# Softmax sums of four head pairs in one matmul group, and their inverses spread by broadcast DMAs

## The chip, the cores and the metric

The kernel runs on one core of one Trainium2 chip. The metric is the device time in microseconds (us) of one execution; three executions of the kernel before took 481.07, 482.66 and 483.11 us, so its median is 482.66 us. A profile is taken of one further execution.

## The reference

Linformer attention on 8 batches, 8 heads, 1024 tokens and head size 64, followed by a feed-forward layer with a squared ReLU (8192 tokens, 512 features, 2048 hidden):

```python
k_proj = einsum('ks,bhsd->bhkd', E, k)             # 1024 keys projected to 64
v_proj = einsum('ks,bhsd->bhkd', F, v)
scores = q @ k_proj.T / sqrt(64)
attn   = exp(scores - max) / (sum(exp(scores - max)) + 1e-9)
x      = (attn @ v_proj) as (8192, 512)
h      = maximum(x @ w_in, 0)
out    = (h * h) @ w_out
```

The kernel leaves out the maximum, which changes nothing of the quotient, and computes the inverse of a sum as exp(-ln(sum)) on ScalarE (ACT).

## The kernel before

**Attention.** A batch has four head pairs. For each, `scores` (L352) makes four 64x64 matmuls into a PSUM tile of two banks (`ps_att`) and ACT writes the exponentials into `expT` (L343, four buffers). The 64 keys of a head lie on 64 partitions, so the softmax sum runs over partitions: a matmul with a matrix of ones gives it. `sums` and `sums_spread` do this for two pairs at once (eight matmuls, 64 rows by 32 columns), which leaves each sum on 32 partitions, 32 copies of one row. The multiply in `values` (L396, L409) needs it on 64. In `sums` (batch 0's second half and batch 1) ACT makes the inverse twice and VectorE (DVE) copies 32 partitions four times (L373). In `sums_spread` (batches 2 to 7) ACT makes `inv` once (L386, L387) and eight DMAs of SyncE's queue copy `inv` into two tiles `rs` of 128 partitions (L393), each from 32 partitions to 32. `inv` and `rs` share one tag with three buffers.

**Feed-forward.** Both products of a chunk of 512 tokens are done as seven half-size products in place of eight, with sums of the operands made on DVE (`sum_x`, `sum_h`), PSUM copies on ACT (L544, L662, L677) and sums with a kept product on DVE (L666). Kept products are tiles `u` of `part_pool`, finished rows are tiles `o_sb` of `out_pool`, stored by SyncE (L566).

**Order.** The order on TensorE (PE) is written out by hand; on the other engines a scheduler places instructions by program order and by when it takes them to be ready. From chunk (1, 1) on a loop of steps runs: each step is one first-layer product (four matmuls of 128x256, L652) and one second-layer quantum (four, L572). A batch has 56 steps. `on(t + n, b, name)` hangs an attention stage behind step n of a batch's period. In the loop there is one PSUM pair for attention, so its stages follow each other through it. Of batch b+2, counted from the period of batch b, the kernel before has: `transpose_q_dma` at 2, `project` at 30, `transpose_k_dma` at 32, `scores` at 44, 47 and 53 and at 1 of the next period, `sums_spread` at 50 and at 3 of the next period; there `values` follow at 7, 10, 20 and 23 and both `sum_x` at 24. Q of a further batch is loaded at 3, K and V at 34, on GpSimd's (POOL) queue.

```python
on(t + 44, b + 2, "scores", 0)
on(t + 47, b + 2, "scores", 1)
on(t + 50, b + 2, "sums_spread", 0)
on(t + 53, b + 2, "scores", 2)
```

Batch 1's attention runs inside chunk (0, 1), batch 2's scores inside chunk (1, 0) (`first_plain`, 16 steps).

Of the kernel before, what the change touches and what calls it, by code (L numbers as in the profile page):

```python
# [9 lines left out]
P = 128  # L10
F32 = mybir.dt.float32
BF16 = mybir.dt.bfloat16
AF = mybir.ActivationFunctionType
ALU = mybir.AluOpType
PE = mybir.EngineType.PE
LO, HI = slice(0, 64), slice(64, 128)
# [3 lines left out]
def kernel(  # L20
# [11 lines left out]
    nc = tc.nc  # L32

    B, H, S, D = q.shape
# [3 lines left out]
    DM = moe_w_out.shape[1]  # L38
# [6 lines left out]
    TCH = S // 2  # L45
# [10 lines left out]
    const_pool = ctx.enter_context(tc.tile_pool(name="const", bufs=1))  # L56
# [4 lines left out]
    soft_pool = ctx.enter_context(tc.tile_pool(name="soft", bufs=3))  # L61
    x_pool = ctx.enter_context(tc.tile_pool(name="x", bufs=2))
    form_pool = ctx.enter_context(tc.tile_pool(name="form", bufs=1))
    part_pool = ctx.enter_context(tc.tile_pool(name="part", bufs=5))
    out_pool = ctx.enter_context(tc.tile_pool(name="outp", bufs=3))
    psum = ctx.enter_context(tc.tile_pool(name="ps", bufs=1, space=bass.MemoryType.PSUM))
    turn = {"att": 0, "bank": 0, "pairs": 2}

# [6 lines left out]
    def att_psum():  # L75
        turn["att"] += 1
        return pair_psum(turn["att"] % turn["pairs"])

    def bank(shape=(P, 512), dtype=F32, n=None):
        if n is None:  # L80
            turn["bank"] += 1
            n = turn["bank"]
        return psum.tile(list(shape), dtype, tag=f"bank{n % 4}", name="ps_bank")
# [34 lines left out]
    nc.vector.memset(zeros[:], 0.0)  # L118
    ones = const_pool.tile([P, D], BF16, name="ones")
    nc.vector.memset(ones[:], 1.0)  # L120


    W_IN_PIECES = ((0, 2), (2, 4), (4, 8), (8, 12), (12, 16))
# [3 lines left out]
    for j, (lo, hi) in enumerate(W_IN_PIECES):  # L127
        t = wpool.tile([P, NCB, (hi - lo) * P], BF16, name=f"w_in_{lo}")
# [6 lines left out]
    for j in range(WP):  # L135
        if j == WP - 1:
            load(Q0[:, :, 4:8, :], tokens(q, 0, i=slice(4, 8)))
        t = wpool.tile([P, fn, DM], BF16, name=f"w_out_{j}")
# [81 lines left out]
    VALUE_QUADS = ((LO, 0, 0, LO), (HI, 0, 1, HI), (HI, 1, 1, LO), (LO, 1, 0, HI))  # L220

    class Attention:
# [31 lines left out]
        def project(self):  # L254
            ps = att_psum()[:, 0]
            for i in range(NI):
                f, l = i == 0, i == NI - 1
                nc.tensor.matmul(ps[LO, :], lhsT=ET[:, i, :], rhs=self.K[:, :, i, :], start=f, stop=l)
                nc.tensor.matmul(ps[HI, :], lhsT=FT[:, i, :], rhs=self.V[:, :, i, :], start=f, stop=l)
            for g in range(2):  # L260
                self.keep_k(ps[LO, g * C // 2:(g + 1) * C // 2], g)
            self.keep_v(ps[HI, :])
# [91 lines left out]
            self.scores_mm(ps, pr, slice(0, NT))  # L354
            self.e[pr] = self.exponentials(ps)

        def sums(self, pr):

            ps = att_psum()
            for j in range(2):  # L360
                for o, par, a, r in VALUE_QUADS:
                    c = 32 * (2 * a + j)
                    nc.tensor.matmul(
                        ps[c:c + 32, par], lhsT=ones[r, 0:32], rhs=self.e[pr + j][r, par], start=True, stop=True
                    )
            rs = [soft_pool.tile([P, 2, TCH], F32, tag="rs", name="rs") for _ in range(2)]
            nc.scalar.activation(rs[1][:], ps[:], AF.Ln)
            nc.scalar.activation(rs[0][:], rs[1][:], AF.Exp, scale=-1.0)
            nc.scalar.activation(rs[1][:], rs[1][:], AF.Exp, scale=-1.0)
            for j in range(2):  # L370
                for a in range(2):
                    have, lack = 32 * (2 * a + j), 32 * (2 * a + 1 - j)
                    nc.vector.tensor_copy(rs[j][lack:lack + 32], rs[j][have:have + 32])  # L373
                self.rs[pr + j] = rs[j]

        def sums_spread(self, pr):

            ps = att_psum()
            for j in range(2):
                for o, par, a, r in VALUE_QUADS:  # L380
                    c = 32 * (2 * a + j)
                    nc.tensor.matmul(
                        ps[c:c + 32, par], lhsT=ones[r, 0:32], rhs=self.e[pr + j][r, par], start=True, stop=True
                    )
            inv = soft_pool.tile([P, 2, TCH], F32, tag="rs", name="inv")
            nc.scalar.activation(inv[:], ps[:], AF.Ln)  # L386
            nc.scalar.activation(inv[:], inv[:], AF.Exp, scale=-1.0)  # L387
            for j in range(2):
                rs = soft_pool.tile([P, 2, TCH], F32, tag="rs", name="rs")
                for a in range(2):  # L390
                    have = 32 * (2 * a + j)
                    for to in (64 * a, 64 * a + 32):
                        nc.sync.dma_start(rs[to:to + 32], inv[have:have + 32])  # L393
                self.rs[pr + j] = rs

        def values(self, pr, spare=False):  # L396

# [40 lines left out]
    class Chunk:  # L438
# [100 lines left out]
                        yield  # L539


        def keep(self, ps):
            u = part_pool.tile([P, DM], F32, name="u")
            nc.scalar.copy(u[:], ps)  # L544
            return u

# [31 lines left out]
        def second_spread(self, second_bank):  # L578
# [21 lines left out]
            yield  # L600
            yield from product(7, chain)
            self.put(1, 1, chain, p5)
            yield
            yield from product(3, other)
# [6 lines left out]
        def second_seven(self, first, chain, other, last=False):  # L611
# [16 lines left out]
            yield  # L628
            yield from product(7, chain)
            self.put(1, 1, chain, p5)  # L630
            yield
            yield from product(3, other)
# [10 lines left out]
    class Group:  # L643
# [35 lines left out]
        def p5(self):  # L679
            self.other = bank(n=turn["bank"] + 2)  # L680
            self.product(5, self.other, True)
            self.kept5 = self.chunk.keep(self.other[:])

        def p6(self):
            self.product(6, self.chain)
            self.u2 = self.chunk.keep(self.chain[:])

        def p2(self):
            self.product(2, self.first)
# [18 lines left out]
    with tc.manual_schedule(engines={PE}):  # L708
# [30 lines left out]
        def at(step, fn, *args, **kwargs):  # L739
            plan.setdefault(step, []).append(lambda: fn(*args, **kwargs))  # L740

        def run(steps, start=0):
            for step, _ in enumerate(steps, start + 1):
                for stage in plan.pop(step, []):
                    stage()
            return step

        def run_all(*parts):
            step = 0
            for part in parts:  # L750
                step = run(part, step)
            assert not plan, plan

        atts = {0: att}
        chunk = {(0, c): Chunk(att, c) for c in range(2)}
# [7 lines left out]
        nxt = atts[1]  # L763
# [23 lines left out]
        at(44, nxt.transpose_q, 2)  # L787
        at(44, nxt.transpose_q, 3)
        at(44, lambda: atts[2].load_q())
        at(45, nxt.sums, 0)  # L790
        at(47, nxt.scores, 2)
        at(49, nxt.scores, 3)
        at(50, nxt.values, 0)
        at(52, nxt.values, 1)
        at(53, nxt.sums, 2)
        at(59, nxt.values, 2)
        at(60, nxt.values, 3)
        at(60, chunk[1, 1].sum_x)
# [5 lines left out]
        run_all(chunk[0, 0].first_cold(), chunk[0, 0].second_cold(), chunk[0, 1].first_plain(), chunk[0, 1].second_seven(*(bank()[:] for _ in range(3))))  # L804

        nxt = atts[2]
        at(1, nxt.transpose_k)
        at(3, nxt.scores, 0)
        at(5, nxt.scores, 1)
        at(7, nxt.sums_spread, 0)  # L810
        at(9, nxt.scores, 2)
        at(11, nxt.scores, 3)
        turn["pairs"] = 1
        run_all(chunk[1, 0].first_plain())
        lent.close()
        second_pool = ctx.enter_context(tc.tile_pool(name="ps_second", bufs=1, space=bass.MemoryType.PSUM))
# [37 lines left out]
        def both():  # L854
            f, s = firsts(), seconds()
            for _ in f:
                next(s, None)
                yield

        def on(step, b, name, *args):  # L860
            at(step, lambda: getattr(atts[b], name)(*args))

        for b in range(1, B - 1):
            t = 56 * (b - 1)
            if b > 1:
                on(t + 1, b + 1, "scores", 3)
            on(t + 3, b + 1, "sums_spread", 2)
            on(t + 7, b + 1, "values", 0)
            on(t + 10, b + 1, "values", 1)
            on(t + 20, b + 1, "values", 2)  # L870
            on(t + 23, b + 1, "values", 3)
            for c in range(2):
                at(t + 24, lambda b=b, c=c: chunk[b + 1, c].sum_x())
            if b + 2 < B:
                on(t + 2, b + 2, "transpose_q_dma")
                if b + 3 < B:
                    at(t + 2, begin, b + 3)
                    on(t + 3, b + 3, "load_q")
                on(t + 30, b + 2, "project")
                on(t + 32, b + 2, "transpose_k_dma")  # L880
                if b + 3 < B:
                    on(t + 34, b + 3, "load_kv")
                on(t + 44, b + 2, "scores", 0)
                on(t + 47, b + 2, "scores", 1)
                on(t + 50, b + 2, "sums_spread", 0)
                on(t + 53, b + 2, "scores", 2)
        steps = both()
        run(steps)
        assert not plan, plan
# [31 lines left out]
```

## Time and profile before

| | |
|---|---|
| median of three executions | 482.66 us |
| profiled execution, device time | 482.35 us |
| its span, first to last instruction | 480.5 us |
| PE busy | 470.4 us, 98% |
| DVE busy | 350.7 us, 73% |
| ACT busy | 287.2 us, 60% |
| one period of 56 steps (186.65 to 242.50, 242.50 to 298.35, 298.35 to 354.20) | 55.85 us each |
| DMA, mean rate | 139 GB/s |
| DMAs from `inv` to `rs` | 96, 128 KB each, 2.8 us from issue to landing (median; 2.2 to 8.9) |

Matmuls are pipelined, and the profile models their ends, so the busy share of PE is an upper bound of its work. Shares and counts are of one execution. A wait is put down to the event that came last.

### The profile page before, as it was taken

Reading aid. Unit: us, or ns where it says so; the run is one execution under the profiler, and the core shown is the slowest. Engines: PE = TensorE matmul, PEld = TensorE weight load, DVE = VectorE, ACT = ScalarE, POOL = GpSimd, SP = SyncE. Lnnn points to the kernel's source line nnn. Section 1 sums busy time; section 2 is a strip of 40 time slices with the busy share of each in tenths; the row PEclk is TensorE's granted clock in tenths of the full one; section 3 lists DMA queues with packets and bytes.
Section 4 is the critical chain, followed back from the end, with each engine's and each line's share of the span. In section 5 each row is a group of like instructions: output and inputs, shape, how many; then the busy total and the mean of one; then the engine's idle time right before and its main releaser. Section 6 shows DMA issues by size and latency. Waiting matters only on the chain.

```text
span 480.5 us, 10027 instructions
## 1 busy us (share of the span) xinstructions
PE 470.4 (98%) x4106; PEld 351.5 (73%) x4106; DVE 350.7 (73%) x613; ACT 287.2 (60%) x466; POOL 32.4 (7%) x45
## 2 busy tenths in 40 slices
PE   8999999999999999999999999999999999999996
PEld 3444445537878788787878778887887778888885
DVE  2456897956996679767897579966797678967671
ACT  2464467397547774678546785477745775565641
POOL 7310010200010000100010000100000000000000
PEclk9999999999999999999999999999999999999999
DMA  9999998999949496767939499495811054101012
GB/s 184 204 205 206 221 164 150 168 230 189 197 86 168 122 201 163 119 134 186 196 103 182 93 220 175 96 160 139 203 56 55 23 132 111 67 23 67 24 65 89
DMA packets 80046, 66.98 MB, mean 139 GB/s; under 512 B 30720, under 2 KB 76032, under 8 KB 80000
## 3 DMA queue, kind: packets, MB, share of 16 engines
q0 software_dynamic: 30640, 29.23, 39.4%
q1 hardware_dynamic: 49216, 36.97, 29.2%
q8 instruction: 32, 0.52, 0.4%
q10 hardware_dynamic: 144, 0.13, 0.1%
q14 instruction: 14, 0.11, 0.1%
HBM read 59.24 MB, written 16.78 MB: 158 GB/s over the span
## 4 chain that ended last, share of the span: by engine, by line
PE 71%; DVE 22%; ACT 3%; issue 2%; DMA 1%; DVEq 0%; ACTq 0%
PE ps_bank L652 28%; PE ps_second L572 27%; PE ps_bank L489 6%; DVE h L150 3%; DVE x_sum L150 3%; DVE h L666 3%; DVE s L150 2%; PE ps_att L329 2%; DVE xT L409 2%; PE ps_second L549 2%; PE ps_att L405 2%; DVE kp L246 1%; DVE rs L373 1%; DVE kp L247 1%; DVE w_in_sum L150 1%
## 5 line engine op out<-in xcount | busy, mean ns | idle before, releaser
L150 DVE TENSOR_TENSOR h<-h 128x1024 bf16<-128x1024 bf16 (+1 forms) x182 | 108.0, 616 | 39.1 <-ACT h L662 25.4
L652 PE MATMUL ps_bank<-x_sum,w_in_sum 128*128 128x256 bf16 x624 | 93.9, 273 | 0.0
L652 PEld LDWEIGHTS <-w_in_sum 128*128 128x128 bf16 x832 | 78.7, 98 | 16.2 <-issue 7.5
L572 PEld LDWEIGHTS <-h 128*128 128x128 bf16 x832 | 80.8, 98 | 10.6 <-DVE h L150 0.2
L662 ACT ACTIVATE h<-ps_bank 128x512 bf16<-128x512 f32 x104 | 62.9, 605 | 28.5 <-PE ps_bank L652 28.3
L544 ACT COPY u<-ps_bank 128x512 f32<-128x512 f32 x107 | 63.2, 591 | 26.6 <-PE ps_bank L652 23.6
L666 DVE CUSTOM_DVE_ANT_0 h<-ps_bank,u 128x512 bf16<-128x512 f32 x104 | 68.9, 685 | 13.0 <-PE ps_bank L652 12.5
L652 PEld LDWEIGHTS <-w_in 128*128 128x128 bf16 x624 | 58.8, 98 | 16.2 <-issue 9.5
L677 ACT COPY ps_bank<-ps_bank 128x512 f32<-128x512 f32 x52 | 29.7, 570 | 66.1 <-PE ps_bank L652 66.1
L572 PEld LDWEIGHTS <-s 128*128 128x128 bf16 x624 | 61.0, 98 | 7.1
L652 PE MATMUL ps_bank<-xT,w_in 128*128 128x256 bf16 x416 | 62.5, 273 | 0.0
L572 PE MATMUL ps_second<-w_out_sum,s 128*128 128x256 bf16 x416 | 62.4, 273 | 0.0
L572 PE MATMUL ps_second<-w_out_sum,h 128*128 128x256 bf16 x416 | 62.2, 273 | 0.0
L572 PE MATMUL ps_second<-w_out,h 128*128 128x256 bf16 x416 | 60.3, 273 | 0.0
L409 DVE TENSOR_TENSOR xT<-ps_att,rs 128x512 bf16<-128x512 f32 x56 | 36.0, 684 | 15.9 <-PE ps_att L405 15.9
L489 PE MATMUL ps_bank<-xT,w_in 128*128 128x512 bf16 x192 | 45.3, 379 | 1.8 <-DVE xT L434 1.0
L485 ACT ACTIVATE h<-ps_bank 128x512 bf16<-128x512 f32 x48 | 28.1, 606 | 16.1 <-PE ps_bank L489 15.9
L150 DVE TENSOR_TENSOR o_sb<-ps_second,u 128x512 f32<-128x512 f32 x27 | 18.5, 684 | 25.9 <-PE ps_second L572 20.7
L489 PEld LDWEIGHTS <-w_in 128*128 128x128 bf16 x192 | 17.7, 98 | 24.6 <-issue 6.2
L343 ACT ACTIVATE expT<-ps_att 128x1024 bf16<-128x1024 f32 x32 | 32.9, 1036 | 2.9 <-PE ps_att L329 2.5
L652 PE MATMUL ps_bank<-x_sum,w_in 128*128 128x256 bf16 x208 | 31.4, 273 | 1.4 <-DVE h L666 1.4
L652 PE MATMUL ps_bank<-xT,w_in_sum 128*128 128x256 bf16 x208 | 31.3, 273 | 0.0
(104 smaller groups left out, 477.2 us busy)
## 6 DMA issues: line engine op xcount, KB each, us to landing
out_dram<-o_sb SPq DMA_DIRECT2D x63, 256.0 KB, 2.4
rs<-inv SPq DMA_DIRECT2D x96, 128.0 KB, 2.8
K_sb<-in_k_dram POOLq DMA_DIRECT2D x7, 1024.0 KB, 9.5
V_sb<-in_v_dram POOLq DMA_DIRECT2D x7, 1024.0 KB, 15.8
Q_sb<-in_q_dram POOLq DMA_DIRECT2D x7, 1024.0 KB, 12.6
w_out<-in_moe_w_out_dram POOLq DMA_DIRECT2D x4, 512.0 KB, 17.9
w_in<-in_moe_w_in_dram POOLq DMA_DIRECT2D x3, 512.0 KB, 15.0
k_f<-in_k_dram SPq DMA_DIRECT2D x1, 512.0 KB, 4.9
```

Of the source, the lines that this page charges most:

```text
L150: return nc.vector.tensor_tensor(out=o, in0=x, in1=y, op=op)
L329: nc.tensor.matmul(ps[o, par], lhsT=self.kT[r, h % 4, h // 4, :], rhs=self.qT[r, h, n, :], start=True, stop=True)
L343: nc.scalar.activation(e[:], ps[:], AF.Exp, scale=SCALE)
L409: nc.vector.tensor_tensor(out=self.xT[:, pr, :, par], in0=ps_x[par].rearrange("p (c t) -> p c t", c=2), in1=rs[:, par].rearrange("p (c t) ...
L485: nc.scalar.activation(h, ps.rearrange("p (a t) -> p a t", a=2), AF.Relu)
L489: nc.tensor.matmul(ps[:], lhsT=w_in_blk(cb, fb), rhs=self.xT[:, cb, self.c].rearrange("p a t -> p (a t)"), start=(cb == 0), stop=(cb == NC ...
L544: nc.scalar.copy(u[:], ps)
L572: nc.tensor.matmul(ps[:, i * HM:(i + 1) * HM], lhsT=self.h_form(n, fb)[:, i * P:(i + 1) * P], rhs=w_out_form(n, fb), start=fresh and i == ...
L652: nc.tensor.matmul(ps[:, j * HC:(j + 1) * HC], lhsT=w_in_form(n, cb, 2 * self.g + j), rhs=self.chunk.x_form(n, cb), start=fresh and j == 0 ...
L662: nc.scalar.activation(self.out(kh, a), ps[:], AF.Relu)
L666: nc.vector._custom_dve(TENSOR_ADD_SAT, out=self.out(kh, a), in0=ps[:], in1=more[:], s0=3.0e38, s1=0.0)
L677: nc.scalar.copy(self.chain[:], self.first[:])
```

## The change

Sums of all four pairs of a batch are made together (`sums_all`): 16 matmuls whose left operand `pick` has 16 columns of ones and 16 of zeros, two of them accumulated into each block of 32 partitions, so that a sum lies on 16 partitions. One `Ln` and one `Exp` make one tile `inv`, which has a tag of its own with one buffer. `spread` then fills `rs` with four DMAs a pair. Each reads one row of `inv` (one partition, 512 floats) 64 times and writes 64 partitions. Batch 1's first two pairs use the same DMAs in place of the copies on DVE (`sums(0, True)`). The plan of the steps is changed with it: all scores stand ahead of the sums, `project` and `transpose_k_dma` move to 49 and 50, K and V are loaded there, Q at 26, `values` go to 6, 9, 19 and 22, the second `sum_x` to 33, and stages of batches 1 and 2 move by a step. `part_pool` has two tags of two buffers in place of five buffers, `out_pool` two in place of three.

```diff
-    part_pool = ctx.enter_context(tc.tile_pool(name="part", bufs=5))
-    out_pool = ctx.enter_context(tc.tile_pool(name="outp", bufs=3))
+    part_pool = ctx.enter_context(tc.tile_pool(name="part", bufs=2))
+    out_pool = ctx.enter_context(tc.tile_pool(name="outp", bufs=2))
...
+    pick = const_pool.tile([P, 2, 32], BF16, name="pick")
+    nc.vector.memset(pick[:], 0.0)
+    for m in range(2):
+        nc.vector.memset(pick[:, m, 16 * m:16 * m + 16], 1.0)
...
-        def sums(self, pr):
+        def sums(self, pr, by_dma=False):
...
+            if by_dma:
+                self.inverse_of(ps)
+                for j in range(2):
+                    self.spread_rows(pr + j, {(par, a): (32 * (2 * a + j), par) for o, par, a, r in VALUE_QUADS})
+                return
...
-        def sums_spread(self, pr):
+        def sums_all(self):
             ps = att_psum()
...
+            for m in range(2):
+                for j in range(2):
+                    for o, par, a, r in VALUE_QUADS:
+                        c = 32 * (2 * j + par)
+                        nc.tensor.matmul(
+                            ps[c:c + 32, 0 if r == LO else 1], lhsT=pick[r, m], rhs=self.e[2 * m + j][r, par],
+                            start=m == 0, stop=m == 1, skip_group_check=True,
+                        )
+            self.inverse_of(ps)
+
+        def inverse_of(self, ps):
+            self.inv = soft_pool.tile([P, 2, TCH], F32, tag="inv", name="inv", bufs=1)
+            nc.scalar.activation(self.inv[:], ps[:], AF.Ln)
+            nc.scalar.activation(self.inv[:], self.inv[:], AF.Exp, scale=-1.0)
+
+        def spread(self, pr):
+            m, j = divmod(pr, 2)
+            self.spread_rows(pr, {
+                (par, a): (32 * (2 * j + par) + 16 * m, 0 if r == LO else 1) for o, par, a, r in VALUE_QUADS
+            })
+
+        def spread_rows(self, pr, at):
+            rs = soft_pool.tile([P, 2, TCH], F32, tag="rs", name="rs")
+            for o, par, a, r in VALUE_QUADS:
+                row, n = at[par, a]
+                nc.sync.dma_start(rs[o, par], self.inv[row:row + 1, n].unsqueeze(1).broadcast_to((1, 64, TCH)))
+            self.rs[pr] = rs
...
-        at(45, nxt.sums, 0)
-        at(47, nxt.scores, 2)
-        at(49, nxt.scores, 3)
-        at(50, nxt.values, 0)
-        at(52, nxt.values, 1)
-        at(53, nxt.sums, 2)
+        at(45, nxt.sums, 0, True)
+        at(48, nxt.scores, 2)
+        at(50, nxt.scores, 3)
+        at(51, nxt.values, 0)
+        at(53, nxt.values, 1)
+        at(54, nxt.sums, 2)
...
-        at(7, nxt.sums_spread, 0)
...
+        on(13, 2, "sums_all")
+        for pr in range(4):
+            on(13, 2, "spread", pr)
...
+        def project(step, b):
+            on(step, b, "project")
+            on(step + 1, b, "transpose_k_dma")
+            if b + 1 < B:
+                at(step + 1, begin, b + 1)
+                on(step + 1, b + 1, "load_kv")
+
+        project(24, 3)
         for b in range(1, B - 1):
             t = 56 * (b - 1)
...
+            for pr, step in enumerate((7, 10, 19, 22) if b == 1 else (6, 9, 19, 22)):
+                on(t + step, b + 1, "values", pr)
             for c in range(2):
-                at(t + 24, lambda b=b, c=c: chunk[b + 1, c].sum_x())
+                at(t + 23 + 10 * c, lambda b=b, c=c: chunk[b + 1, c].sum_x())
             if b + 2 < B:
-                on(t + 2, b + 2, "transpose_q_dma")
+                on(t + 12, b + 2, "transpose_q_dma")
                 if b + 3 < B:
...
+                    on(t + 26, b + 3, "load_q")
+                    project(t + 49, b + 3)
+                for pr in range(4):
+                    on(t + 37 + 3 * pr, b + 2, "scores", pr)
+                on(t + 53, b + 2, "sums_all")
+                for pr in range(4):
+                    on(t + 53, b + 2, "spread", pr)
```

More of the change, by code (lines that the diff above doesn't have):

```diff
@@ L374, in sums @@
                 self.rs[pr + j] = rs[j]
-        def sums_spread(self, pr):
+        def sums_all(self):
             ps = att_psum()
[L379 to L394, printed above, removed]
+            for m in range(2):
[22 more added lines that the diff above has]
+            self.rs[pr] = rs
         def values(self, pr, spare=False):
@@ L539, in second_cold, with keep @@
                         yield
-        def keep(self, ps):
-            u = part_pool.tile([P, DM], F32, name="u")
+        def keep(self, ps, tag="second"):
+            u = part_pool.tile([P, DM], F32, name="u", tag=tag)
             nc.scalar.copy(u[:], ps)
@@ L681, in p5 @@
             self.product(5, self.other, True)
-            self.kept5 = self.chunk.keep(self.other[:])
+            self.kept5 = self.chunk.keep(self.other[:], "first")
         def p6(self):
             self.product(6, self.chain)
-            self.u2 = self.chunk.keep(self.chain[:])
+            self.u2 = self.chunk.keep(self.chain[:], "first")
         def p2(self):
@@ L806 @@
         nxt = atts[2]
-        at(1, nxt.transpose_k)
-        at(3, nxt.scores, 0)
-        at(5, nxt.scores, 1)
-        at(7, nxt.sums_spread, 0)
+        at(2, nxt.transpose_k)
+        at(4, nxt.scores, 0)
+        at(6, nxt.scores, 1)
         at(9, nxt.scores, 2)
@@ L813, with on @@
         turn["pairs"] = 1
+        def on(step, b, name, *args):
+            at(step, lambda: getattr(atts[b], name)(*args))
+        on(13, 2, "sums_all")
+        for pr in range(4):
+            on(13, 2, "spread", pr)
         run_all(chunk[1, 0].first_plain())
@@ L858, in both @@
                 yield
-        def on(step, b, name, *args):
-            at(step, lambda: getattr(atts[b], name)(*args))
+        def project(step, b):
[5 more added lines that the diff above has]
+        project(24, 3)
         for b in range(1, B - 1):
             t = 56 * (b - 1)
[L865 to L871, printed above, removed]
+            for pr, step in enumerate((7, 10, 19, 22) if b == 1 else (6, 9, 19, 22)):
+                on(t + step, b + 1, "values", pr)
             for c in range(2):
-                at(t + 24, lambda b=b, c=c: chunk[b + 1, c].sum_x())
+                at(t + 23 + 10 * c, lambda b=b, c=c: chunk[b + 1, c].sum_x())
             if b + 2 < B:
-                on(t + 2, b + 2, "transpose_q_dma")
+                on(t + 12, b + 2, "transpose_q_dma")
                 if b + 3 < B:
[L877 to L886, printed above, removed]
+                    on(t + 26, b + 3, "load_q")
[5 more added lines that the diff above has]
+                    on(t + 53, b + 2, "spread", pr)
         steps = both()
```

## The prediction

> **What bounds the kernel now.** I read the page's busy times first, then the three steady periods as stretches, then TensorE's timeline in one of them, then who waited for whom in it.
>
> ```profile
> span 480.5 us, 10027 instructions
> PE 470.4 (98%) x4106; PEld 351.5 (73%) x4106; DVE 350.7 (73%) x613; ACT 287.2 (60%) x466; POOL 32.4 (7%) x45
> ...
> 242.50:298.35 55.85, 55.56 (x514) 44.78 (x513) 43.41 (x74) 35.78 (x59) 2.62 (x3) 1.00 0.76 152
> ...
> 268.44 0.60 PE L652 MATMUL ps_bank<-xT,w_in 128*128 128x256 bf16 x4
> 268.88 0.60 PE L572 MATMUL ps_second<-w_out,s 128*128 128x256 bf16 x4
> 269.41 0.41 PE L382 MATMUL ps_att<-expT,ones 64*32 64x512 bf16 x8
> 269.75 0.61 PE L652 MATMUL ps_bank<-x_sum,w_in_sum 128*128 128x256 bf16 x4
> ...
> PE ps_bank L652 <- DVE h L666: 0.3, 1, 0.3
> ```
>
> The stretch's columns are length, then PE, weight loads, DVE, ACT, POOL, clock and DMA share. PE is busy for 55.56 of 55.85 us, at the full clock. In the timeline starts matter: four feed-forward matmuls take 268.88 - 268.44 = 0.44 us, but 0.53 ahead of a sums block, and the block of eight 0.34. So a sums block costs 0.34 + 0.09 = 0.43 us (0.45 with the slower start behind it). PE's only wait of note in the period is 0.3 us for DVE. PE bounds the kernel; a step is 55.85 / 56 = 1.00 us. DVE (43.4 us) runs close behind: a long DVE wait becomes PE's, since PE's next PSUM bank is freed by L666.
>
> The change works on the chain sums, inverse, spread, multiply. Timelines of ACT and SyncE:
>
> ```profile
> 269.89 1.02 ACT L386 ACTIVATE inv<-ps_att 128x1024 f32<-128x1024 f32 x1 [0.19 <-PE ps_att L382]
> 271.27 1.07 ACT L387 ACTIVATE inv<-inv 128x1024 f32<-128x1024 f32 x1
> ...
> 272.37 6.14 SPq L393 DMA_DIRECT2D rs<-inv  x8
> ```
>
> Three us after the sums start, eight DMAs are issued, 0.77 us each; the page gives 2.8 us to landing. How they use the DMA engines shows in two short stretches: first 273.50 to 276.00 with spread DMAs alone, then 2.55 to 3.10 with the load of E (from HBM to 64 partitions, 4 KB packets).
>
> ```profile
> DMA packets 173, 0.52 MB, mean 210 GB/s; under 512 B 48, under 2 KB 48, under 8 KB 172
> q1 hardware_dynamic: 172, 0.51, 89.5%
> ...
> q1 hardware_dynamic: 39, 0.15, 68.1%
> ```
>
> In the first, 172 - 48 = 124 data packets fill 0.895 x 16 engines x 2.5 us, 289 ns each. In the second, 38 data packets (one of the 39 is small) fill 0.681 x 16 x 0.55 us, 158 ns each. A packet of 4 KB takes nearly twice as long when 16 engines read it from 32 partitions.
>
> [...] 16 x 4096 B / 289 ns = 227 GB/s[...].
>
> **The change part by part.** The sum is made against the span of 480.5 us; the profiled run took 482.35, the median is 482.66, so 2.2 us lie around it.
>
> *PE.* Twelve sums blocks become six of 16 matmuls. Eight run in 0.34 us, 0.21 of it their own stream (512 columns at the 0.107 us per 256 that the 0.44 us per four imply), so a block of 16 costs 0.45 + 0.21 = 0.66. Saved: 12 x 0.45 - 6 x 0.66 = 1.4 us, on the path. *ACT.* 12 x (1.02 + 1.06) = 25 us become half; ACT is at 64% of a period, PE covers it: nothing by itself. *DVE.* Four copies of 0.685 us in batch 1 go (2.7 us); PE waited 0.5 us for DVE there. K's casts (four of 0.41) and the second `sum_x` (four of 0.42) leave steps 24 to 33, where DVE ran without a break before the 0.3 us wait; five such waits are 1.4 us. Together at most 1.9, at worst they reappear at step 50: I take 1. *Buffers.* A store lands in 2.4 us and finished tiles come at least four steps apart; kept products need two at a time: nothing, while stores aren't held up. *Moved stages.* K's transpose (8.6 us to landing) goes from 32 to 50, needed 43 steps later; Q's stands in the built order behind the last scores, needed some 40 later; loads of K and V get 55 steps as against 52, Q's some 40 as against 55, with 12.6 us to landing: nothing. But K's transpose now stands just ahead of the spreads in SyncE's queue, and all 16 spreads ahead of the next stores.
>
> *The spreads.* Still 16 DMAs of 128 KB a batch, but each reads one partition. The trace shows no such read. Lower bound: like the DMAs before, 128 KB / 227 GB/s = 0.6 us each. [...] I let nothing overlap. I take 4.8[...].
>
> Then, with inverses 3.2 us after the sums and 2.2 us of each 2.8 us landing being fixed, the pairs land 3.2 + 2.2 + 19.2 = 24.6, 43.8, 63.0 and 82.2 us after the sums. The multiplies are planned 9, 12, 22 and 25 steps after them. The last wants 25 us and gets 82: 57 us lost. It is lost in four pieces (15.6, 16.2, 9.2, 16.2), since DVE takes its queue in order: behind each multiply stand sums and squares for which PE waits within a step or two. The fourth pair's DMAs wait for a buffer from the first multiply, and the stores stand behind them; both fall inside these waits. Some 1 us of each batch's loss is covered by DVE's lead. Six batches: 6 x 56 = 336 us. Batch 1's eight DMAs end 3.2 + 2.2 + 38.4 = 44 us after the sums, planned for 8 steps of about 1 us: 35 us. Sum: 480.5 - 1.4 - 1 + 336 + 35 = 849, with 2.2 around it **851 us**.
>
> **The rivals.** *The read of one row is no slower than that of 32* (0.6 us a DMA; the other side). [...] Against it: the doubled packet time. Then 16 issues of 0.77 us are the pace, the first pair lands 3.2 + 3 x 0.77 + 2.8 = 8.3 us after the sums against 9 planned, and what is left is -1.4 and between 0 and -1.9: 479.4 to 481.3, say **480 us**. It decides below about 0.7 us a DMA.
>
> *The read is quick, but the spread comes late.* The margin is 0.7 us, K's transpose stands just ahead, and landings went up to 8.9 us. With 1 to 4 us late in each of six batches: 480.3 + 6 to 24, **486 to 504 us**, say 494. Against it: most landings took 2.8.
>
> [...] 9.6 us a DMA, 154 us a batch: each batch loses 134, batch 1 74, **1360 us**. Nothing in the profile speaks for it.
>
> **How the numbers follow.** The first case has 0.60. Its own range is 740 (four fifths of the time a DMA: 61 us for 16, a loss of 41 a batch and 28 in batch 1) to 960 (loads and stores share the engines and add a quarter: 19 more a batch). The quick and timely read has 0.19, the late one 0.17, half rate 0.04. About 0.5% or 2.4 us is what can be told from no change: the quick case lies at -0.3 to -0.7%, so 0.11 faster and 0.08 same; slower has 0.81. To hold 8 in 10 the range must reach into both: 479 to 960.
>
> **What would show it.** In the profile after, the group of spreads (L414) must show landings of 20 us and more, packets of 2 KB of about 1.2 us[...], and DVE's multiplies (L430) must wait for DMAs for some 50 us a batch, with a period near 112 us. The PE part is right if a block of 16 sums takes 0.55 us from its start to the next group's. The quick read would show landings near 3 us, 2 KB packets of about 0.15 us and a period of 55.3 to 55.7. [...]

## The result and the profile after

The changed kernel takes 813.26 us (median of four executions, 807.76 to 814.15); the kernel before took 482.65 us beside it (481.07 to 483.11). The ratio is 1.684, with a 95% interval of 1.677 to 1.691. The forecast of 851 us was 38 us too high.

The page of the changed kernel: span, busy times, the group of multiplies, and the issues of spreads (count, size, median us from issue to landing).

```profile
span 806.0 us, 10067 instructions
...
PE 522.5 (65%) x4096; PEld 376.6 (47%) x4106; DVE 349.7 (43%) x612; ACT 277.2 (34%) x453; POOL 32.4 (4%) x45
...
L430 DVE TENSOR_TENSOR xT<-ps_att,rs 128x512 bf16<-128x512 f32 x56 | 38.0, 688 | 270.4 <-DMA rs<-inv 270.4
...
rs<-inv SPq DMA_DIRECT2D x104, 128.0 KB, 15.9
```

PE is busy for 65% of the span in place of 98%. DVE waits 270.4 us for spreads, ahead of multiplies that themselves still take 688 ns. The median landing went from 2.8 to 15.9 us.

One steady period as a stretch, from the first long wait of PE in one batch to that in the next (columns as in the prediction):

```profile
356.01:461.35 105.34, 65.69 (x515) 49.73 (x512) 43.61 (x73) 34.33 (x58) 2.62 (x3) 0.77 0.79 83
```

The period is 105 us in place of 55.85. The work in it is the same: 515 matmuls and 43.6 us of DVE, against 514 and 43.4. PE's 65.7 us are the same matmuls at a lower clock (0.77), and the other 40 us are waiting. Who waited for whom in the whole span (us in total, times, longest):

```profile
DVE xT L430 <- DMA rs<-inv: 270.4, 42, 13.2
...
PE ps_att L426 <- DVE xT L430: 127.2, 13, 20.4
...
DVE o_sb L154 <- DMA out_dram<-o_sb: 73.3, 5, 15.3
PE ps_bank L673 <- DVE h L687: 68.0, 8, 12.1
PE ps_second L593 <- DVE o_sb L154: 54.1, 5, 11.5
```

DVE's wait reaches PE by three ways. A second multiply holds the attention PSUM pair, so PE waits for L430 (127.2 us). Or L687 (L666 in the kernel before), queued behind a multiply, holds a feed-forward bank (68.0 us). Or DVE waits behind the spreads in SyncE's queue (the third line): finished rows can't be stored, with two `o_sb` buffers the next one waits, and PE waits for its bank (54.1 us, once in each of batches 3 to 7).

SyncE's timeline shows why. The 16 issues of a batch took 12 us before (two groups of eight, about 6 us each); they now take 59.48 us:

```profile
347.81 59.48 SPq L414 DMA_DIRECT2D rs<-inv  x16
```

In this batch the trace has the sums at 344.63 us and the last DMA of the four pairs landing as below. Within a pair the landings stand 4.4 to 4.9 us apart, but the last DMA of a pair comes only 3.5, 2.3, 0.8 and 1.8 us after the one ahead of it.

| pair landed, us after the sums | first | second | third | fourth |
|---|---|---|---|---|
| forecast | 24.6 | 43.8 | 63.0 | 82.2 |
| measured | 25.7 | 42.5 | 57.8 | 73.1 |

PE's timeline behind one of the waits (start, us, then engine and line):

```profile
389.67 1.01 PE L673 MATMUL ps_bank<-x_sum,w_in_sum 128*128 128x256 bf16 x4 [9.87 <-DVE h L687]
390.48 1.06 PE L593 MATMUL ps_second<-w_out_sum,s 128*128 128x256 bf16 x4
391.33 1.06 PE L673 MATMUL ps_bank<-x_sum,w_in 128*128 128x256 bf16 x4
...
394.52 0.60 PE L673 MATMUL ps_bank<-xT,w_in 128*128 128x256 bf16 x4
394.96 0.60 PE L593 MATMUL ps_second<-w_out_sum,h 128*128 128x256 bf16 x4
```

After the 9.87 us of waiting, four matmuls take 0.85 us (390.48 to 391.33); from 394.52 on they take 0.44 again. PE ran at half rate for some 4.6 us (granted clock 0.50 from 389.7 to 394.3).

### The profile page after: what moved, and what is told of

The parts are those of the page before. It is cut to its first block, busy times and chain, and to the rows that moved or that the text cites. A ratio compares the mean times of both kernels' runs of the same rounds, so it can differ in the third digit from the quotient of the medians.

```text
span 806.0 us, 10067 instructions
## 1 busy us (share of the span) xinstructions
PE 522.5 (65%) x4096; PEld 376.6 (47%) x4106; DVE 349.7 (43%) x612; ACT 277.2 (34%) x453; POOL 32.4 (4%) x45
## 3 DMA queue, kind: packets, MB, share of 16 engines
q1 hardware_dynamic: 52928, 38.02, 54.7%
## 4 chain that ended last, share of the span: by engine, by line
PE 34%; SPq 27%; DMA 27%; DVE 8%; ACT 2%; issue 2%; DVEq 0%; ACTq 0%; POOLq 0%
SPq L414 27%; DMA rs<-inv 17%; PE ps_bank L673 12%; PE ps_second L593 12%; DMA out_dram<-o_sb 10%; PE ps_bank L510 4%; PE ps_att L262 2%; PE ps_att L333 1%; DVE h L154 1%; DVE xT L430 1%; DVE o_sb L154 1%; PE ps_second L570 1%; DMA K_sb<-in_k_dram 1%; DVE w_in_sum L154 1%; DVE w_out_sum L154 1%
## 5 line engine op out<-in xcount | busy, mean ns | idle before, releaser
L430 DVE TENSOR_TENSOR xT<-ps_att,rs 128x512 bf16<-128x512 f32 x56 | 38.0, 688 | 270.4 <-DMA rs<-inv 270.4
L673 PE MATMUL ps_bank<-x_sum,w_in_sum 128*128 128x256 bf16 x624 | 107.1, 300 | 68.0 <-DVE h L687 68.0
L673 PEld LDWEIGHTS <-w_in_sum 128*128 128x128 bf16 x832 | 86.0, 106 | 93.8 <-issue 77.8
L593 PEld LDWEIGHTS <-h 128*128 128x128 bf16 x832 | 84.7, 102 | 68.4 <-issue 54.9
L593 PE MATMUL ps_second<-w_out_sum,h 128*128 128x256 bf16 x416 | 70.0, 296 | 54.1 <-DVE o_sb L154 54.1
L683 ACT ACTIVATE h<-ps_bank 128x512 bf16<-128x512 f32 x104 | 62.2, 598 | 110.2 <-PE ps_bank L673 109.0
L426 PE MATMUL ps_att<-expT,vp 64*64 64x512 bf16 x112 | 14.7, 516 | 127.2 <-DVE xT L430 127.2
L593 PEld LDWEIGHTS <-s 128*128 128x128 bf16 x624 | 68.9, 110 | 15.0
L673 PEld LDWEIGHTS <-w_in 128*128 128x128 bf16 x624 | 64.0, 106 | 20.3 <-issue 8.6
L593 PE MATMUL ps_second<-w_out_sum,s 128*128 128x256 bf16 x416 | 73.4, 307 | 0.0
L687 DVE CUSTOM_DVE_ANT_0 h<-ps_bank,u 128x512 bf16<-128x512 f32 x104 | 69.1, 684 | 8.4 <-PE ps_bank L673 6.9
L673 PE MATMUL ps_bank<-xT,w_in 128*128 128x256 bf16 x416 | 65.9, 283 | 0.0
L593 PE MATMUL ps_second<-w_out,h 128*128 128x256 bf16 x416 | 60.1, 272 | 0.0
L154 DVE TENSOR_TENSOR o_sb<-ps_second,u 128x512 f32<-128x512 f32 x27 | 18.5, 687 | 87.5 <-DMA out_dram<-o_sb 73.3
L673 PE MATMUL ps_bank<-x_sum,w_in 128*128 128x256 bf16 x208 | 38.8, 320 | 0.0
L593 PE MATMUL ps_second<-w_out,s 128*128 128x256 bf16 x208 | 36.9, 308 | 0.0
L673 PE MATMUL ps_bank<-xT,w_in_sum 128*128 128x256 bf16 x208 | 34.2, 291 | 0.0
## 6 DMA issues: line engine op xcount, KB each, us to landing
rs<-inv SPq DMA_DIRECT2D x104, 128.0 KB, 15.9
w_in<-in_moe_w_in_dram POOLq DMA_DIRECT2D x3, 512.0 KB, 14.4
```

The lines of the kernel that those rows point to most:

```text
L154: return nc.vector.tensor_tensor(out=o, in0=x, in1=y, op=op)
L426: nc.tensor.matmul(ps_x[par][o], lhsT=self.vp[r, 2 * pr + a, :], rhs=e[r, par], start=True, stop=True)
L430: nc.vector.tensor_tensor(out=self.xT[:, pr, :, par], in0=ps_x[par].rearrange("p (c t) -> p c t", c=2), in1=rs[:, par].rearrange("p (c t) ...
L593: nc.tensor.matmul(ps[:, i * HM:(i + 1) * HM], lhsT=self.h_form(n, fb)[:, i * P:(i + 1) * P], rhs=w_out_form(n, fb), start=fresh and i == ...
L673: nc.tensor.matmul(ps[:, j * HC:(j + 1) * HC], lhsT=w_in_form(n, cb, 2 * self.g + j), rhs=self.chunk.x_form(n, cb), start=fresh and j == 0 ...
L683: nc.scalar.activation(self.out(kh, a), ps[:], AF.Relu)
```

## The experiments

Two theories stood at first. The *port* theory, a guess that no trace had shown then: a partition is read through something that it shares with its neighbours, called a port here, and this alone sets the 4.4 to 4.9 us between landings, however many DMA engines read. The *plan* theory: the moved stages and the smaller pools cost the time, and the slow spreads are a consequence.

**The kernel before, with one-row reads.** Everything stays as it was, but each spread reads one row for its 32 partitions.

```diff
-                        nc.sync.dma_start(rs[to:to + 32], inv[have:have + 32])
+                        nc.sync.dma_start(rs[to:to + 32], inv[have:have + 1].unsqueeze(1).broadcast_to((1, 32, 2, TCH)))
```

> The kernel before with one thing changed: each of its 96 spread DMAs reads one row of inv 32 times in place of 32 rows with the same values; every engine's order stays the same. Port theory[...]: 128 KB take 4.8 us, less where the next DMA is at another port, and the time goes to 740 to 830 us. Plan theory (the new order of stages and the 16 spreads in one go lose the time): no change, 480 to 485 us. Row theory (it is the repeated row or the zero step, whatever the port): as the port theory.

One execution took 728.62 us, with these landings (2.8 us in the median before):

```profile
rs<-inv SPq DMA_DIRECT2D x96, 128.0 KB, 12.9
```

The old plan, order and pools don't save it: 246 us of the 331 come with this one edit. It was 11 us under the range expected. The plan theory falls as the main cause.

**Rows one apart, or four apart.** Sums lie on 16 partitions each, so a pair's four DMAs can read different copies of their row. In one run DMA i reads the row i partitions further (all within the groups of four partitions that the change reads in), in the other 4i further. Packets, bytes and order are otherwise those of the change.

```diff
-            for o, par, a, r in VALUE_QUADS:
+            for i, (o, par, a, r) in enumerate(VALUE_QUADS):
                 row, n = at[par, a]
+                row += 1 * i        # the other run: 4 * i
```

> The changed kernel, but the four DMAs of a pair read four different rows with the same values that lie next to each other (row, row + 1, + 2, + 3[...]). Port theory: as the changed kernel, 806 to 816 us, a DMA each 4.1 us on average. Row theory (one partition's reads are what is served slowly): the four DMAs overlap as those of the third run do, below 700 us. Plan theory: 806 to 816.

> The changed kernel, but the four DMAs of a pair read rows 4 apart (row, row + 4, + 8, + 12[...]). Port theory: every DMA has another port than the one ahead of it, so the overlap seen between pairs (1 to 3 us in place of 4.8 between landings) comes at each, some 35 us for 16 DMAs, 580 to 680 us. Row theory: the same as the second run. Zero-step theory (the form of the read, one row 64 times): 806 to 816 us.

One execution each: 809.85 us with steps of one partition, 594.89 us with steps of four, both within what the port theory expected. DVE's wait for the spreads, first with steps of one:

```profile
DVE xT L431 <- DMA rs<-inv: 267.5, 41, 10.1
```

and with steps of four:

```profile
DVE xT L431 <- DMA rs<-inv: 96.6, 31, 7.2
```

Other partitions of the same four are worth nothing (DVE waits 267.5 against 270.4 us); other groups of four are worth 215 us of the whole time. So it isn't the repeated read as such that is slow, but what the four neighbouring partitions share; *port* is no more than a name for that here. Rows 32 apart share it too: in the change a pair's first two DMAs read one row and its third the row 32 further, and in the batch shown the third landing stands 4.4 to 4.8 us behind the second.

**Sixteen rows in one DMA.** Each DMA reads its sum from all 16 partitions that hold it, four times each, in place of one partition 64 times. They are four such groups of four neighbours. Every engine's order stays that of the change.

```diff
-                nc.sync.dma_start(rs[o, par], self.inv[row:row + 1, n].unsqueeze(1).broadcast_to((1, 64, TCH)))
+                nc.sync.dma_start(rs[o, par], self.inv[row:row + 16, n].unsqueeze(1).broadcast_to((16, 4, TCH)))
```

> The changed kernel, but each DMA reads 16 rows with the same values four times each, with as many packets, DMAs and bytes as before, and the same order on every engine. Port theory: 16 rows lie on four ports, so a DMA takes 1.2 us, the pairs land 10, 15, 20 and 25 us after the sums against 9, 12, 22 and 25 planned, and the kernel takes 490 to 515 us. Plan theory and zero-step theory: near 810 us.

It took 507.70 us (four executions, 507.47 to 509.48), 1.054 times the kernel before (1.051 to 1.057). The wait for spreads:

```profile
DVE xT L430 <- DMA rs<-inv: 43.2, 24, 4.2
```

So 813.3 - 507.7 = 306 us of the change's loss of 331 come from reading a single row. What remains, 26 us (against 481.61 us of the kernel before, measured beside it), has another cause, and the timelines ahead of one batch's spreads name suspects. SyncE's:

```profile
166.14 4.86 SPq L325 DMA_TRANSPOSE qT<-Q_sb  x1
171.09 0.54 SPq L587 DMA_DIRECT2D out_dram<-o_sb  x1
172.28 1.29 SPq L299 DMA_TRANSPOSE kT<-kp  x1
175.03 0.38 SPq L587 DMA_DIRECT2D out_dram<-o_sb  x1
177.38 14.65 SPq L414 DMA_DIRECT2D rs<-inv  x10
```

and GpSimd's, with the loads:

```profile
170.96 0.88 POOL L89 DMA_DIRECT2D K_sb<-in_k_dram  x1 [25.34 <-PE ps_att L263]
171.83 0.88 POOL L89 DMA_DIRECT2D V_sb<-in_v_dram  x1
173.38 0.88 POOL L89 DMA_DIRECT2D Q_sb<-in_q_dram  x1 [0.66 <-DMA qT<-Q_sb]
```

Three loads of 1 MB and two transposes are issued in the 11 us ahead of the spreads; the first spread lands 9.4 us after its issue (186.77, from the trace). `project` at step 49 is what frees the buffers of K and V just then. The batches of this run tell the loads from the transposes. Batch 6 has both transposes ahead of its spreads (347.60 and 353.71 us) but no loads, and its first spread lands 3.3 us after its issue, as in batch 7, which has neither just ahead. In batches 3 to 5, with loads, it takes 8.2 to 9.4 us. So the loads delay the spreads; the transposes alone do not.

To see where time is lost I lined up the starts of the 2,912 feed-forward matmuls in the loop of steps (L673 and L593, L652 and L572 before), which all these kernels run in one order. How far each kernel lies behind the kernel before, in its profiled execution, us:

| | loop begins | batch 2 done | 3 | 4 | 5 | 6 | end |
|---|---|---|---|---|---|---|---|
| the change | 16.4 | 75.8 | 127.8 | 177.3 | 229.0 | 275.8 | 324.6 |
| sixteen rows | 3.8 | 13.2 | 18.7 | 22.6 | 27.1 | 24.8 | 24.3 |
| + projections at 24 | 0.1 | 9.3 | 10.6 | 12.9 | 14.7 | 15.3 | 15.0 |
| + SyncE as written | 10.0 | 11.9 | 12.6 | 13.2 | 13.9 | 14.4 | 14.0 |
| + later multiplies | 9.7 | 10.0 | 10.7 | 11.0 | 11.5 | 11.8 | 11.2 |
| + Q's transpose at 55 | 1.9 | 2.4 | 2.7 | 3.6 | 4.3 | 5.3 | 5.1 |
| with batch 1 on DVE | 3.7 | 4.5 | 4.9 | 6.0 | 6.6 | 7.2 | 6.9 |
| with projections at 27 | 3.2 | 3.3 | 3.4 | 3.5 | 3.9 | 4.0 | 3.6 |

"Batch n done" is the start of the first of these matmuls behind its 56 steps (448 matmuls). The other rows are the next runs, each built on the one above it, but the last two both on the run with Q's transpose at 55.

**Projections at step 24.**

```diff
-        project(24, 3)
         for b in range(1, B - 1):
             t = 56 * (b - 1)
+            if b + 2 < B:
+                project(t + 24, b + 2)
...
-                    project(t + 49, b + 3)
```

> Sixteen-row spreads as in the run before, and the projections of every batch at step 24 of a period instead of 49, so that the loads of K and V and K's transpose are issued some 27 steps ahead of the spreads instead of just before them; nothing else is changed. Theory A (the rest of the loss, 507.7 less 481.6 = 26 us, comes from the loads and the transpose that stand on the same DMA engines ahead of the first spread): the first spread lands 4 to 6 us after its issue in place of 9, the waits of 3 to 4.5 us of TensorE for the first multiply of each of the five steady batches go, and the time falls by 12 to 20 us, to 488 to 496 us; batches 1 and 2 keep their waits (3 and 5 us). Theory B (the spreads themselves, or the sums made late, are what is late): the first landing stays near 9 us after the issue, and the time stays at 504 to 510 us.

501.04 us (498.08 to 501.62), 1.038 times the kernel before (1.034 to 1.042): between the two ranges. The loads cost something: PE's waits for the first multiply of batches 3 to 5 fell from 3.1 to 4.2 us to 1.1 to 1.8, and the first spread landed 6.4 us after its issue in place of 9.4. What is left of that delay is a load of Q, which starts when Q's transpose frees its buffer, about 2 us ahead of the spreads of these batches:

```profile
171.44 0.88 POOL L89 DMA_DIRECT2D Q_sb<-in_q_dram  x1 [26.78 <-DMA qT<-Q_sb]
173.46 18.53 SPq L414 DMA_DIRECT2D rs<-inv  x16
```

Batch 6 has such a transpose too (337.18 us) but no load behind it, and there the first spread lands in 3.4 us. But batch 2 still lost 9.2 us. SyncE's timeline there:

```profile
104.44 9.37 SPq L325 DMA_TRANSPOSE qT<-Q_sb  x1
113.91 10.92 SPq L414 DMA_DIRECT2D rs<-inv  x11
```

The inverse was finished at 109.34 (its `Exp` starts at 108.29 and takes 1.05). SyncE was busy issuing Q's transpose until 113.91.

**Batch 1's first pairs on DVE.** Built on the run with the projections at 24.

```diff
-        at(45, nxt.sums, 0, True)
+        at(45, nxt.sums, 0)
...
-            for pr, step in enumerate((7, 10, 19, 22) if b == 1 else (6, 9, 19, 22)):
+            for pr, step in enumerate((9, 12, 19, 22) if b == 1 else (6, 9, 19, 22)):
```

> The run with the projections at step 24, and besides batch 1's first two pairs on VectorE's copies as in the kernel before, and batch 2's first two multiplies at steps 9 and 12 of the period in place of 7 and 10. Theory A (what is left after the loads are moved are the waits of batches 1 and 2): 3 to 8 us less than the run with the projections alone, 482 to 490 us. Theory B (the rest is spread over the steady batches): less than 2 us of difference.

499.90 us (498.51 to 501.65): 1 us less, within the spread of both. A miss for the theory that batches 1 and 2 could be mended in this way.

**SyncE in written order.** The scheduler puts Q's transpose ahead of the spreads, since it becomes ready when the last scores free `qT`. In the program's own order it stands behind them.

```diff
-    with tc.manual_schedule(engines={PE}):
+    with tc.manual_schedule(engines={PE, mybir.EngineType.SP}):
```

> The run with sixteen rows and the projections at step 24, with SyncE's queue in the order in which the program issues it, instead of the scheduler's: Q's transpose then stands behind the 16 spreads of a batch instead of ahead of them. VectorE, ScalarE and TensorE keep their order. Theory A (batch 2's spreads are late because SyncE is held up 4.6 us by the issue of Q's transpose, and the steady ones because the transpose's data still runs when they are issued): batch 2's spreads are issued as soon as the inverses are there, its loss falls from 8.4 to about 3 us, the steady batches lose under 1 us in place of 1 to 2, and the time is 489 to 495 us. Theory B (the sums simply come too late for the multiplies at step 6): 498 to 503 us as before.

497.17 us (495.56 to 497.92), 1.030 times (1.028 to 1.033): above the 489 to 495 expected. Inside the loop the loss falls as theory A has it: the first spread of the batch at 176.03 lands 3.3 us after its issue, and the loop loses 4.0 us in place of 14.9. But in the steady batches it was not the transpose's data that came in the way, as the theory said: by batch 6 of the earlier run it was the load of Q, and the written order moved that behind the spreads too (203.79 us for the batch at 176.03). And the kernel is 10 us late before the loop begins, by a wait that the written order brought:

```profile
PE ps_att L333 <- DMA qT<-Q_sb: 5.8, 1, 5.8
```

Batch 2's transpose of Q is written at step 61, behind three stores, and PE waits for it from 99.3 to 105.1 us. One queue's order was mended at one place and broken at another.

**The first two multiplies later.**

```diff
-            for pr, step in enumerate((7, 10, 19, 22) if b == 1 else (6, 9, 19, 22)):
+            for pr, step in enumerate((9, 12, 19, 22) if b == 1 else (8, 11, 19, 22)):
```

> The run before this one, with the first two multiplies of every batch 2 steps later (9 and 12 of batch 2's period, 8 and 11 of the others). Theory A (once the port, the loads, and the transpose are out of the way, what is left is a fixed latency from sums to the first multiply): the waits of TensorE for the first multiply go altogether, and the time is that of the kernel before less the 1 to 2 us that fewer sums are worth, 479 to 485 us. Theory B (the multiplies are not what is left): within 2 us of the run before.

494.67 us (492.47 to 497.65), 1.026 times (1.023 to 1.029). That is 2.5 us less than the run before, in which PE's waits at the multiplies in the loop had already fallen to at most 1.1 us. The loop now loses 1.5 us in place of 4.0. The total expected was wrong by the 9.7 us before the loop, which I had left out of it.

**Q's transpose at step 55.**

```diff
-        at(61, lambda: atts[2].transpose_q_dma())
+        at(55, lambda: atts[2].transpose_q_dma())
```

> The run with later multiplies, and Q's transpose of batch 2 issued at step 55 of the first chunks instead of 61, so that it stands ahead of three stores in SyncE's queue, as the scheduler had it in the runs before the written order. Theory A (the 9.7 us that the run with later multiplies has lost when the loop of steps begins are TensorE's wait of 5.1 us for this transpose, the half rate behind it, and the wait for batch 1's first spread): the wait of 5.1 us goes, 6 to 8 us less, 486 to 490 us. Theory B (the loss before the loop has another cause): 492 to 496 us.

487.20 us (484.71 to 489.08), 1.011 times (1.008 to 1.013). The wait is gone, and the loop begins 1.9 us late. Two stretches of 56 us in the loop:

```profile
166.00:222.00 56.00, 55.30 (x513) 44.70 (x511) 43.10 (x74) 33.88 (x58) 2.63 (x3) 1.00 0.91 154
222.00:278.00 56.00, 54.73 (x507) 44.19 (x506) 42.95 (x73) 33.30 (x57) 2.63 (x3) 1.00 0.89 149
```

PE is busy for 54.7 to 55.3 us of 56 at the full clock: it is the bound again.

**Two attempts on the last 5 us.** Batch 1's first pairs on DVE's copies again, on this base (the first diff), and the projections at 27, so that PE doesn't wait for the last multiply ahead of them (the second).

```diff
-        at(45, nxt.sums, 0, True)
+        at(45, nxt.sums, 0)
```

> The run with Q's transpose at step 55, and batch 1's first two pairs spread by VectorE's copies as in the kernel before, instead of by DMAs. What is left of the change is the sums of four pairs and their spread, from sixteen rows, for batches 2 to 7. Theory A (batch 1's DMAs cost TensorE a wait of about 2 us and the half rate behind it): 2 to 4 us less than the run before this one, 482 to 487 us. Theory B (VectorE's copies cost as much as the DMAs): within 2 us of it.

```diff
-                project(t + 24, b + 2)
+                project(t + 27, b + 2)
...
-                    on(t + 26, b + 3, "load_q")
+                    on(t + 29, b + 3, "load_q")
```

> The run with Q's transpose at step 55, and the projections at step 27 of a period instead of 24, five steps behind the last multiply instead of two (loads of Q at 29). Theory A (what is left per batch, 0.6 us, is mostly TensorE's wait of 0.4 to 1.1 us ahead of the projection, for the last multiply to free the PSUM pair): five waits go, 2 to 4 us less, 483 to 485.5 us. Theory B (that wait is not on the path that sets the end): within 1.5 us of 487.

486.73 us (483.50 to 489.97; 1.009, 1.006 to 1.013) and 487.19 us (484.70 to 489.78; 1.011, 1.007 to 1.015). By their times neither can be told from the base. The single profiled executions say more. PE's waits in the base, then in the run with the projections at 27:

```profile
PE ps_att L262 <- DVE xT L430: 3.6, 5, 1.1
PE ps_att L367 <- DVE xT L430: 2.7, 1, 2.7
...
PE ps_bank L673 <- DVE h L687: 3.0, 5, 0.6
PE ps_att L367 <- DVE xT L430: 2.5, 1, 2.5
```

With the projections at 27, the waits of 0.4 to 1.1 us ahead of them are gone, and a wait of 0.6 us for L687 stands 14 steps further in each period. By the table the loop now loses 0.4 us in place of 3.2. The 3.2 us that are left at its beginning hold PE's wait for batch 1's first spread (L367). With DVE's copies that wait is gone, but this execution, the slowest of its seven, lost time at the start. The first 20 us in the run with copies, then with the projections at 27 (the last columns are clock, DMA share and rate):

```profile
0.00:20.00 20.00, 16.25 (x96) 7.93 (x97) 4.96 (x15) 5.46 (x6) 12.66 (x22) 0.74 1.12 190
...
0.00:20.00 20.00, 17.34 (x130) 8.24 (x131) 6.20 (x18) 7.84 (x9) 12.79 (x22) 1.00 1.12 190
```

At its matmul of 68.45 us (64.80 before) it is 3.65 us behind, and 3.7 when the loop begins: between the two it loses nothing, where the base loses 3.0 us (from a matmul at 63.74 us). So each attempt removes about 3 us, one ahead of the loop and one in it, as far as one execution each can show. They were not run together, and why the start differs stays open. No version here beats the kernel before.

## Why the prediction was right

**The spreads' price, right.** The step rested on 4.8 us a DMA with nothing overlapping, the author's estimate, which the trace of before didn't show. Measured are 4.4 to 4.9 us between landings of one pair, and the runs with steps of one and of four partitions (809.85 and 594.89 us) show that neighbouring partitions share what limits them. The rate itself shows in 5 us of batch 6 in which only spreads run (565 to 570 us):

```profile
DMA packets 83, 0.14 MB, mean 27 GB/s; under 512 B 16, under 2 KB 16, under 8 KB 83
q1 hardware_dynamic: 83, 0.14, 90.7%
```

83 - 16 = 67 packets of 2 KB fill 0.907 x 16 engines x 5 us, 1.08 us each (1.2 forecast). The landings of 20 us and more that were named came for a part of the DMAs only (median 15.9, longest 33.9), since a landing is counted from its own issue, and SyncE issued the later ones late. In the batch shown DVE waited 37.5 us for spreads (50 forecast) and 14.2 us more for stores, in a period of 105 us (112 forecast).

**"I let nothing overlap", mis-sized.** It holds within a pair. At each change of pair the work overlaps: the last DMA of a pair landed 0.8 to 3.5 us after the one ahead of it. The 16 DMAs took some 65 us (first landing at 357.19 less 4.8, last at 417.74) and not 16 x 4.8 = 77, so the fourth pair landed 73.1 us after the sums, not 82.2. The first pair's 25.7 us (24.6 forecast) are in part luck: its first DMA landed 2.4 us later than forecast, behind loads, and the overlap gave 1.3 us back. The trace shows this overlap, but no spread that landed before one issued ahead of it. With steps of four partitions, 16 DMAs landed within 26.4 us in one batch (280.53 to 306.97), and within 26 to 32 us in all six: there the work overlaps within a pair too.

**Six batches of 56 us, 28 too many.** The table of delays gives 59.4, 52.0, 49.5, 51.7, 46.8 and 48.8 us, 308 in all. For a steady batch: the fourth pair 73.1 us after the sums, planned 25 steps after them, is 48 us; some 3 us at half rate behind the last wait (seven groups of matmuls at 0.85 us in place of 0.44) make 51. The waits of PE alone (14.9, 9.9, 4.6 and 10.3 us in the batch shown) are only 40, because the rest of the time runs as half rate behind each of them. Behind the wait of 9.87 us shown it lasted some 4.6 us. A shorter wait was enough too: in the run with Q's transpose at 55, half clock (0.50) followed PE's wait of 2.7 us (80.03 to 82.71):

```profile
84.00:87.40 3.40, 3.40 (x18) 2.35 (x17) 2.12 (x4) 2.82 (x4) 0.00 (x0) 0.50 1.16 217
```

The prediction left half rate out and lost little by it, since PE's slow work lies inside the time that DVE waits anyway. Batch 2 is longest; there Q's transpose holds SyncE: 11.28 us of issue from 120.74 on, with the inverse ready at 125.64, which the prediction had not put there.

**Batch 1 at 35 us, mis-sized by half.** The loop begins 16.4 us late. I had let nothing overlap here either. In `sums(0, True)` a pair's two rows lie 64 partitions apart, and not 32 as in the steady batches, and the eight landings (79.19 to 100.26 us) come 4.6 to 5.2 and 0.7 to 2.1 us apart by turns, the last 2.4. The last was 30.6 us after the sums, not 44.

**PE's sums, right.** A block of 16 took 0.56 us from its start to the next group's in six of six cases (0.55 forecast). The stream of 512 columns in that forecast is 0.22 us by the trace of before, not 0.21: four matmuls of 256 start 0.435 us apart (251.33 to 253.07). What this is worth for the whole can't be separated from the rest; no run did the sums alone.

**"Moved stages: nothing; buffers: nothing", wrong.** At the change itself the slow reads hide most of it: the first spread landed 9.4 to 11.1 us after its issue in batches 3 to 5, with loads just ahead, and 6.9 us in batches 6 and 7, without. With sixteen rows it is 26 us, 5.4% of the kernel. The prediction asked of each moved transfer whether it is in time for its own consumer. It noted K's transpose just ahead of the spreads, and left it as a rival ("the spread comes late", 486 to 504 us). In kind that rival came true as the second cause (507.7 us, just above its range), but what delays the steady batches' spreads are the loads, and not K's transpose: batch 6, which has it ahead without loads, isn't delayed. The parts of the 26 us, by the runs: the projections' place with its loads, 6.7 us; the order of SyncE's queue with the multiplies' place and Q's transpose, another 13.8 us; 5 us are left. As for the buffers, the 73.3 us of waiting for stores are there in the change, nearly all within the waits for the spreads as forecast: in the batch shown DVE got its `o_sb` at 418.60 us, 0.9 us after the last spread. The pools were never put back, so their own cost is not shown; in the last runs all that is left of the change's loss is about 5 us.

**The lower end of the first case's range, mis-added.** Its terms for four fifths of the time make 480.5 - 1.4 - 1 + 6 x 41 + 28 + 2.2 = 754 us, not 740.

## What to carry to other kernels

Before a DMA repeats one SBUF row to many partitions, look at how many partitions it reads and how far apart they lie: a broadcast of 128 KB from one partition took 4.4 to 4.9 us here, and about 1.2 us when it was read from the 16 partitions that already held copies. A transfer that is moved must be looked at for whom it stands ahead of, in its queue and among the DMAs in flight (with sixteen rows the first spread landed 3.3 us after its issue without loads ahead, and 8.2 to 9.4 with them), and not only for whether it is itself in time. And where a scheduler places DMA issues, read the order that it made: the transpose of Q that held up batch 2's spreads was written behind them.

## What the runs showed of the hardware that I had not expected

- A DMA of 128 KB from 16 partitions lands every 1.2 us in the mean when nothing stands ahead of it (16 landings from 179.31 to 196.94 us in the run with SyncE in written order, 0.4 to 1.6 us apart): 131,072 B / 1.2 us = 109 GB/s, 4 times the 27 GB/s of one row (131,072 B / 4.8 us).
- SyncE itself is held: a DMA's issue took 0.59 us in the median before, 3.6 in the change, and up to 11.5. A slow transfer thus delays whatever the same engine issues next, stores included (DVE waited 73.3 us for them).
- The issue of one DMA transpose of Q occupies SyncE for 4.8 to 11.3 us in the change (4.2 to 6.5 before), as long as the eight issues of a spread group before (5 to 7 us) or longer.
